# A linear attention and two MLPs on one core: one list scheduler for every queue, eight slices ahead of block 1, attention chunks 4 to 23 in one chain

## The chip, the core and the metric

The kernel runs on one core of a Trainium2 chip. The metric is the device time of one execution in microseconds (us). The core has TensorE (PE, its weight loads shown apart as PEld), VectorE (DVE), ScalarE (ACT), GpSimd (POOL), SyncE (SP, which here only issues transfers) and 16 DMA engines. Every engine runs its own list of instructions in the order in which they were put there; an instruction at the head of a list that waits for another engine holds everything behind it.

## What is computed

The reference, cut to what matters (B = 4, H = 8, S = 768, D = 64; 3072 tokens, d_model 512, d_ff 2048, all float32 in the reference):

```python
for t in range(S):                                   # attention with a decayed state per head
    state = gamma * state + outer(k[:, :, t], v[:, :, t])
    y[:, :, t] = scale * (q[:, :, t] @ state)
x = y as 3072 tokens x 512
h = x @ w_in;  g = h * sigmoid(1.702 * h);                       x = g @ w_out     # first MLP
h = x @ w_in2; g = max(h, 0) + alpha * min(h, 0);              out = g @ w_out2    # second MLP
```

The weights arrive as 64-bit floats. Each product is made of three fp32r products (high by high, low by high, high by low), so each weight is turned into a high and a low part first.

## The kernel before

**Work.** The 3072 tokens are 24 attention chunks of 128 and six blocks of 512. Each MLP's weights are 16 slices of 128 features, each with an `in` and an `out` half. Converting one half takes two ACT passes and four DVE passes over the raw words (`conv_words`, `conv_f32`), then an ACT cast and a DVE subtraction for each of its two pieces `wb` (`conv_hi`, `conv_lo`).

**First part.** `plain()` runs 32 steps; a step is 12 matmuls of 512 columns into `ph` (`mlp_h`), the gate and a high/low split of `g`, and 12 matmuls into four banks `py` (`mlp_y`, one step later). The order is: block 0 on the first LEAD slices, block 1 on all 16, block 0 on the rest. Block 0's partial sums are stored (`part`) and loaded again. Beside that run the conversion of the first MLP's weights, the storing of the pieces for the later part, the sums of pieces that the later part needs (`conv_sums`, `slice_sums`, `conv_split`) and attention chunks 0 to 15.

**Second part.** Blocks 2 to 5 of the first MLP and all of the second MLP are five pairs of blocks (`PAIRS`), computed with seven products in place of eight: 280 units of 6 matmuls (`h_unit`, banks `pa` and `pd`) and 280 chunks of 6 matmuls (`y_chunk`, banks `py`), the chunks 36 units behind. Weight pieces are loaded again from HBM, HRING = 6 units and YRING = 6 chunks ahead. The second MLP's weights are converted here, and attention chunks 16 to 23 are done.

**Attention turns.** From chunk 4 on, `half_step(o, new)` does the output of chunk `o` (32 matmuls of 64x64 into `px`) alternating with the scores and the state update of chunk `new` (32 matmuls into `sc` and `pu`). The table TURN says where; `None` stands for a side that is left out. A turn needs `v_scale(new)`, eight ACT multiplications of 128x64, and that needs the chunk's loads.

**Loads.** Everything but chunks 8 to 15 of attention, and the weights, goes to one of 82 slots of SBUF (`load_early`, four transfers of 256 KB a chunk, tile `early`). Raw weights and chunks 8 to 15 (RINGED) share a ring `ld` of five buffers of 512 KB: a load into it is issued when the load five places earlier has been used up.

**Order.** In the first part a list scheduler (`play`) sets the order of PE, DVE, ACT and SP together: each piece of work is a generator that yields an engine, a time, what it reads and what it writes; the scheduler keeps a clock for each engine, each slot and the DMA, and takes the piece that can start first, or one of a lower rank number that can start within 200 ns of it. In the second part only PE's order is written by hand; the other engines' order is left to the framework's own scheduler, with `tc.high_priority` for some pieces.

Of the kernel before, what the change touches and what calls it, by code (L numbers as in the profile page):

```python
# [35 lines left out]
LEAD = 5  # L36
LAG = 1
WARM = 30
# [4 lines left out]
HP = 300  # L43
HG = 100
# [21 lines left out]
YRING = 6  # L66
# [8 lines left out]
STORE_W = (24, 0.9)  # L75
# [11 lines left out]
def tile_linear_attention_two_mlps(ctx: ExitStack, tc, qk, kv, w1, w2, consts, alpha, out):  # L87
# [59 lines left out]
    chains, number, planning = [], counter(), [True]  # L147
# [54 lines left out]
    def start(gen, rank=0.0):  # L202
        if not planning[0]:
            with tc.high_priority(HG):
                for _ in gen:
                    pass
            return
        chain = [rank, next(number), gen, None]
        if go(chain):
            chains.append(chain)  # L210
# [125 lines left out]

    def conv_all(key):
        for part_ in (conv_words, conv_f32, conv_hi, conv_lo):
            yield from part_(key)

# [66 lines left out]
    def conv_sums(kind, layer, i):  # L407
        pair = (kind, layer, 2 * i), (kind, layer, 2 * i + 1)
        yield lambda: all(k in raw for k in pair)
# [33 lines left out]
    def conv_split(kind, layer, i):  # L443
        yield lambda: (kind, layer, i) in sums
        for name, s in zip(("s1", "s3"), sums.pop((kind, layer, i))):
            ws = []
            for part_ in halves(s):
                ws.append((yield from piece_hi(part_, s)))
# [30 lines left out]
    def v_scale(c):  # L479
        vt = loaded["kv", c][1]  # L480
# [132 lines left out]
    def half_psum(which, c):  # L613
        if c >= 4 * BT // C:
# [3 lines left out]
    def half_products(o, new):  # L618
# [51 lines left out]
        span = {32: 2100, 16: 1150}[len(turns)] / 2  # L670
# [18 lines left out]
    def half_step(o, new):  # L689
        if o is not None:  # L690
            yield lambda: ("a", o) in att and ("mid", o) in att
        if new is not None:
            yield lambda: ("v", new) in att
# [11 lines left out]
        start(half_rest(o, new), 0.1)  # L705
# [33 lines left out]
    def half_x(c):  # L739
        px, key = att.pop(("px", c))  # L740
        px = px.rearrange("p (n i) -> p n i", n=NP)
        t, i = divmod(c % (2 * BT // C), BT // C)
        if c < 2 * BT // C:
            x32 = att["x", c] = take("x32", (P, NP, C))
        for k in range(2):
            for d in range(2):
# [5 lines left out]
                if i == 0:  # L752
                    xl[k, d, t] = take("xl")
                yield V(240, [key], [xl[k, d, t]])
                x_out(xl[k, d, t][:, i * C:(i + 1) * C], px[:, n, :], c, n)
                if i == BT // C - 1:
                    ready.add(("xl", c // (2 * BT // C), k, d, t))
# [18 lines left out]
    def x_load(idx, t):  # L776
        assert ("x", idx) in stored
        for k in range(2):
            for d in range(2):
                xl[k, d, t] = take("xl")  # L780
                nc.sync.dma_start(out=xl[k, d, t], in_=xsd[idx][k, :, d, t])

    def x_prep(idx, n):
# [6 lines left out]
        if idx == 0:  # L790
            yield lambda: n == 0 or ("xp", n - 1) in ready
            yield lambda: all(("xl", 1, k, d, t) in ready for k in range(2) for d in range(2) for t in range(2 if n > 1 else 1))
        for k in range(2):
            if which == "t2":
                t1, t2 = xt[idx, "t1", k], xt[idx, "t2", k] = take("t1"), take("t2")
                yield from sub(t1, xl[k, 0, 1], xl[k, 0, 0])
                yield from sub(t2, xl[k, 1, 1], t1)
                give(xl.pop((k, 0, 0)))
            if which == "t3":
                xt[idx, "t3", k] = take("t3")  # L800
                yield from sub(xt[idx, "t3", k], xl[k, 1, 1], xl[k, 0, 1])
                give(xl.pop((k, 0, 1)))
            if which == "t4":
                xt[idx, "t4", k] = t = xt.pop((idx, "t2", k))
                yield from sub(t, xl[k, 1, 0], t)
                give(xl.pop((k, 1, 0)))
            if which[0] == "b":
                yield from x_split(idx, n, k, xl[k, int(which[1]) - 1, int(which[2]) - 1])
                if which == "b22":
                    give(xl.pop((k, 1, 1)))  # L810
# [4 lines left out]
        if idx == 0:  # L815
            ready.add(("xp", n))
# [7 lines left out]
    def gate(layer, ft, g, src):  # L824
        if layer == 1:
            nc.scalar.activation(out=g, in_=src, func=AF.Gelu_apprx_sigmoid)
            return
        t = take("t")
        nc.scalar.activation(out=t, in_=src, func=AF.Relu, scale=-1.0)  # L829
        nc.scalar.activation(out=g, in_=src, func=AF.Relu)  # L830
        nc.vector.scalar_tensor_tensor(  # L831
# [4 lines left out]
    def g_split(g, keep=False):  # L836
        gh, gl = take("gh", dtype=F32R), take("gl", dtype=F32R)
        nc.scalar.copy(out=gh, in_=g)  # L838
        nc.vector.tensor_tensor(out=gl, in0=g, in1=gh.bitcast(F32), op=ALU.subtract)  # L839
# [29 lines left out]
    def mlp_g(j, ft, ph, key):  # L869
        g = take("g")  # L870
        yield A(480, [key], [g])
        gate(1, ft, g, ph)
        gh, gl = take("gh", dtype=F32R), take("gl", dtype=F32R)
        yield A(505, [g], [gh])
        nc.scalar.copy(out=gh, in_=g)
        yield V(600, [g, gh], [gl])
        nc.vector.tensor_tensor(out=gl, in0=g, in1=gh.bitcast(F32), op=ALU.subtract)
        give(g)
        g_of[1, j, ft] = gh, gl
# [55 lines left out]
    def load_piece(ring, name, kind, layer, i, n):  # L935
# [7 lines left out]
        nc.sync.dma_start(out=dst, in_=src)  # L943
# [28 lines left out]
    def h_unit(u):  # L972
        quad, n = units[u]
        idx, q = divmod(quad, NQ)
        layer = PAIRS[idx][0]
        w = hw.popleft()
        if n == 0:
            chain[quad, "a"] = ps_h.tile([P, BT], F32, tag="h", name="pa")
            chain[quad, "d"] = ps_a.tile([P, BT], F32, tag="a", name="pd")
        ps = chain[quad, "d" if n % 2 else "a"]  # L980
        x = xo[idx, n][0]
        prods = [(part_, 0, k) for k in range(2) for part_ in range(2)] + [(0, 1, k) for k in range(2)]
        for m, (part_, low, k) in enumerate(prods):
# [8 lines left out]
        g = None  # L992
        with tc.high_priority(HP):
            if n in (0, 2, 3):
                chain[quad, n] = take("gw")
                nc.scalar.copy(out=chain[quad, n], in_=ps)  # L996
            elif n in (1, 4, 5):
                g = chain.pop((quad, {1: 0, 4: 3, 5: 2}[n]))
                nc.vector.tensor_tensor(out=g, in0=ps, in1=g, op=ALU.add)  # L999
        if g is not None:  # L1000
            t, odd = {1: (0, 0), 4: (1, 1), 5: (1, 0)}[n]
            with tc.high_priority(HG):
                gate(layer, 2 * q + odd, g, g)
            g_of[idx, t, 2 * q + odd] = g
        if n == 6:
            g = g_of[idx, 0, 2 * q + 1] = take("gw")
            with tc.high_priority(HP):
                gate(layer, 2 * q + 1, g, ps)
        if q == QORD[idx][-1] and idx + 1 < len(PAIRS):
            for _ in x_prep(idx + 1, n):  # L1010
                pass
# [3 lines left out]
    def y_split(c):  # L1015
        with tc.high_priority(HG):
            idx, grp, p, m = ychunks[c]
            f = 2 * QORD[idx][GQ * grp + m]
            b11, b12 = (idx, 0, f), (idx, 1, f)
            b21, b22 = (idx, 0, f + 1), (idx, 1, f + 1)  # L1020
            sub = lambda o, x, y: nc.vector.tensor_tensor(out=o, in0=x, in1=y, op=ALU.subtract)
            which = X_OF[p]
# [394 lines left out]
```

## Time and profile before

| | |
|---|---|
| three runs | 1039.66, 1042.46 (median), 1043.55 us |
| the profiled execution | 1041.78 us, of which the span from the first to the last instruction is 1040.0 us |
| TensorE | busy 1019.2 us (98%), mean granted clock 0.993 |
| VectorE, ScalarE | busy 862.7 us (83%), 677.4 us (65%) |
| DMA | 285.46 MB, 274 GB/s over the span |

The time outside the span is 1.8 us. A busy TensorE is not a TensorE at full rate: a matmul counts as busy from its start to its modelled end, also when the clock is halved. So the busy share alone does not say what is left; the rate at which matmuls follow each other, and the places where one waits, do.

### The profile page before, as it was taken

To read this page: it belongs to the slowest core of one execution; us is meant where nothing else is said; L and a number is where in the kernel's file an instruction comes from. 1 tells how busy PE (TensorE), PEld (TensorE's weight loads), DVE (VectorE), ACT (ScalarE), POOL (GpSimd) and SP (SyncE) were. 2 spreads that over 40 slices of the span, in tenths; PEclk is the share of its full clock that TensorE was granted. 3 is DMA by queue.
4 is the path that set the end of the run, shared out by engine and by line. 5 is a ranking of instruction groups with operands and counts; after the bars stand their busy time and mean duration, and the time that the engine had idled before them with its cause. 6 is when DMAs were issued, how large, how long until landed. Compare 5 with 4: busy or idle time off the path is not lost.

```text
span 1040.0 us, 19858 instructions
## 1 busy us (share of the span) xinstructions
PE 1019.2 (98%) x6910; PEld 842.8 (81%) x6910; DVE 862.7 (83%) x1711; ACT 677.4 (65%) x1407; POOL 2.8 (0%) x6
## 2 busy tenths in 40 slices
PE   8999989999999999999999999999999999999998
PEld 7788878787888888888788888788888888888886
DVE  5979979784559999999899999998677978677792
ACT  6958857556455886765776776775555855556740
POOL 1000000000000000000000000000000000000000
PEclk9999999999999999999999999999999999999999
DMA  9749999997846899999979898986686766775661
GB/s 350 238 146 378 382 350 328 373 312 265 275 135 204 283 314 374 352 391 375 358 246 341 311 318 323 323 290 207 219 283 211 217 215 191 227 250 172 193 202 61
DMA packets 144676, 285.46 MB, mean 274 GB/s; under 512 B 16192, under 2 KB 16576, under 8 KB 144576
## 3 DMA queue, kind: packets, MB, share of 16 engines
q1 hardware_dynamic: 144288, 283.84, 80.5%
q8 instruction: 55, 0.90, 0.4%
q10 hardware_dynamic: 288, 0.35, 0.1%
q14 instruction: 45, 0.37, 0.1%
HBM read 209.68 MB, written 74.45 MB: 273 GB/s over the span
## 4 chain that ended last, share of the span: by engine, by line
PE 84%; DMA 7%; DVE 4%; ACT 4%; issue 1%; SPq 0%; DVEq 0%; ACTq 0%
PE py L1058 34%; PE pa L984 20%; PE pd L984 15%; PE py L900 5%; PE ph L863 5%; DMA ld<-kv 2%; PE px L626 2%; ACT v L485 1%; DMA yw<-wcout 1%; ACT wb L356 1%; DMA wcin<-wb 1%; DMA xsd<-y 1%; DMA ld<-w 1%; DVE wb L361 1%; DVE gl L839 1%
## 5 line engine op out<-in xcount | busy, mean ns | idle before, releaser
L1058 PE MATMUL py<-gh,yw 128*128 128x512 f32 x1120 | 300.5, 390 | 0.0
L1058 PEld LDWEIGHTS py<-gh,yw 128*128 128x128 f32 x1120 | 210.6, 188 | 44.1 <-ACT gh L838 0.3
L984 PE MATMUL pa<-xo,hw 128*128 128x512 f32 x912 | 231.3, 390 | 0.0
L984 PEld LDWEIGHTS pa<-xo,hw 128*128 128x128 f32 x912 | 170.8, 188 | 35.7
L839 DVE TENSOR_TENSOR gl<-gw,gh 128x512 fp32r<-128x512 f32 x240 | 160.8, 687 | 37.2 <-ACT gh L838 33.1
L838 ACT CAST gh<-gw 128x512 fp32r<-128x512 f32 x240 | 145.5, 621 | 61.9 <-PE py L1058 29.9
L984 PE MATMUL pd<-xo,hw 128*128 128x512 f32 x684 | 173.8, 390 | 2.6 <-ACT gw L996 2.6
L1058 PE MATMUL py<-gl,yw 128*128 128x512 f32 x560 | 173.1, 390 | 1.3 <-DVE gl L839 1.3
L984 PEld LDWEIGHTS pd<-xo,hw 128*128 128x128 f32 x684 | 128.6, 188 | 29.9 <-ACT gw L996 3.0
L1058 PEld LDWEIGHTS py<-gl,yw 128*128 128x128 f32 x560 | 105.3, 188 | 23.5 <-DVE gl L839 1.7
L1072 DVE TENSOR_TENSOR yc<-py,yc 128x512 f32<-128x512 f32 x99 | 63.6, 683 | 25.3 <-PE py L1058 25.3
L831 DVE SCALAR_TENSOR_TENSOR gw<-t,nalpha,gw 128x512 f32<-128x512 f32 x96 | 71.2, 747 | 15.6 <-ACT gw L830 15.4
L829 ACT ACTIVATE t<-gw 128x512 f32<-128x512 f32 x72 | 45.5, 632 | 51.6 <-DVE gw L999 46.8
L863 PE MATMUL ph<-xhi,wb 128*128 128x512 f32 x256 | 65.8, 399 | 2.8 <-ACT wb L356 2.1
L900 PE MATMUL py<-gh,wb 128*128 128x512 f32 x256 | 66.0, 400 | 1.3 <-DVE wb L361 1.3
L999 DVE TENSOR_TENSOR gw<-pd,gw 128x512 f32<-128x512 f32 x80 | 54.8, 685 | 6.9 <-PE pd L984 6.8
L996 ACT COPY gw<-pa 128x512 f32<-128x512 f32 x80 | 46.6, 583 | 21.4 <-PE pa L984 20.8
L863 PEld LDWEIGHTS ph<-xhi,wb 128*128 128x128 f32 x256 | 48.4, 191 | 13.6 <-ACT wb L356 2.3
L900 PEld LDWEIGHTS py<-gh,wb 128*128 128x128 f32 x256 | 48.1, 192 | 12.4 <-DVE wb L361 1.8
L356 ACT CAST wb<-cvt 128x256 fp32r<-128x256 f32 x112 | 41.0, 403 | 25.1 <-DVE cvt L334 14.4
L361 DVE TENSOR_TENSOR wb<-s,wb 128x256 fp32r<-128x256 f32 x128 | 48.4, 420 | 10.5 <-ACT wb L356 10.5
L356 ACT CAST wb<-s 128x256 fp32r<-128x256 f32 x128 | 47.5, 403 | 13.0 <-DVE s L421 10.6
(107 smaller groups left out, 1368.0 us busy)
## 6 DMA issues: line engine op xcount, KB each, us to landing
hw<-wcin SPq DMA_DIRECT2D x266, 256.0 KB, 4.4
yw<-wcout SPq DMA_DIRECT2D x232, 256.0 KB, 3.7
ld<-w SPq DMA_DIRECT2D x64, 512.0 KB, 5.8
wcin<-wb SPq DMA_DIRECT2D x112, 256.0 KB, 5.6
wcout<-wb SPq DMA_DIRECT2D x88, 256.0 KB, 5.2
yw<-wo SPq DMA_DIRECT2D x48, 256.0 KB, 5.1
early<-kv SPq DMA_DIRECT2D x32, 256.0 KB, 5.4
early<-qk SPq DMA_DIRECT2D x32, 256.0 KB, 5.6
```

The costliest lines, as they stand in the source:

```text
L356: nc.scalar.copy(out=w[:, 0:256], in_=src)
L361: nc.vector.tensor_tensor(out=w[:, 256:], in0=src, in1=w[:, 0:256].bitcast(F32), op=ALU.subtract)
L831: nc.vector.scalar_tensor_tensor(out=g, in0=t, scalar=nalpha[:, ft:ft + 1], in1=g, op0=ALU.mult, op1=ALU.add)
L838: nc.scalar.copy(out=gh, in_=g)
L839: nc.vector.tensor_tensor(out=gl, in0=g, in1=gh.bitcast(F32), op=ALU.subtract)
L863: nc.tensor.matmul(out=ph, lhsT=cols(w, low, k), rhs=x[:, k, :], start=(n == 0), stop=(n == len(prods) - 1),)
L900: nc.tensor.matmul(out=py[e], lhsT=lhsT, rhs=g, start=(begin and seen[e] == 1), stop=(end and seen[e] == 3))
L984: nc.tensor.matmul(out=ps, lhsT=w[:, 256 * part_ + k * P:256 * part_ + (k + 1) * P], rhs=x[2 * k + low], start=(n in (0, 1, 3) and m == 0) ...
L996: nc.scalar.copy(out=chain[quad, n], in_=ps)
L999: nc.vector.tensor_tensor(out=g, in0=ps, in1=g, op=ALU.add)
L1058: nc.tensor.matmul(out=ps[e], lhsT=w[:, at:at + P], rhs=t, start=(fresh and seen[e] == 1), stop=(m == GQ - 1 and seen[e] == 3), skip_group ...
L1072: add_ = lambda o, x: nc.vector.tensor_tensor(out=o, in0=ps, in1=x, op=ALU.add)
```

## The change

- All queues of both parts are ordered by the one list scheduler: `h_out`, `gate`, `g_split`, `y_split`, `y_out` and the loads of the second part become generators with engines and times, or go through `dma()`, which keeps the scheduler's clock of the DMA; `plain` and `streamed` are one lead chain for PE. `high_priority` and the framework's order are gone.
- LEAD goes from 5 to 8.
- TURN has no `(x, None)`, `(None, y)` pair between chunk 4 and chunk 23 any more: 21 turns for 23.
- RINGED is empty: chunks 8 to 15 are loaded in slots too. From chunk 17 on a chunk's loads are issued 24 units ahead of its turn, not 14. YRING goes from 6 to 5.
- All eight `out` sums are made from the converted words (RAW_OUT), so `slice_sums` is not used. Sums and stores of the first MLP are due earlier. The second MLP's conversions begin before the second part, and wait for free slots (SPARE).
- At the start there are 10 small matmuls for 30, then 18 on a tile of zeros, and five of 512 columns ahead of the first step (FILL).

```diff
-LEAD = 5
+LEAD = 8
-WARM = 30
+WARM = 10
+FILL = 5
-YRING = 6
+YRING = 5
-SUMS_IN = (16, 24, 32, 38, 40, 43, 45, 46)
-SUMS_OUT = (12, 20, 28, 36, 41, 48, 50, 52)
-RAW_OUT = (0, 1, 2, 3, 4)
+SUMS_IN = (14, 17, 20, 23, 30, 34, 38, 41)
+SUMS_OUT = (15, 18, 21, 24, 32, 36, 40, 43)
+RAW_OUT = range(8)
-RINGED = range(8, 16)
+RINGED = ()
-W2_AT = [9 + 0.86 * m for m in range(18)] + [26 + 1.25 * m for m in range(14)]
-TURN = ((None, 4, 0), (4, 5, 2), (5, 6, 4), (6, 7, 5), (7, None, 7))
-TURN += ((None, 8, 35), (8, 9, 37), (9, 10, 38), (10, 11, 42), (11, 12, 44), (12, 13, 46), (13, 14, 48), (14, 15, 50))
-TURN += ((15, None, 52), (None, 16, 2), (16, 17, 6), (17, 18, 10), (18, 19, 14), (19, 20, 18), (20, 21, 27))
-TURN += ((21, 22, 30), (22, 23, 33), (23, None, 36))
-FETCH = 14
+W2_AT = [-2 + 1.4 * m for m in range(8)] + [10 + 1.3 * m for m in range(24)]
+TURN = ((None, 4, 0), (4, 5, 8), (5, 6, 10), (6, 7, 12), (7, 8, 14))
+TURN += ((8, 9, 34), (9, 10, 36), (10, 11, 39), (11, 12, 43), (12, 13, 45), (13, 14, 48), (14, 15, 50), (15, 16, 52))
+TURN += ((16, 17, 7), (17, 18, 10), (18, 19, 14), (19, 20, 18), (20, 21, 28), (21, 22, 31), (22, 23, 34), (23, None, 36))
+FETCH = 24
+SPARE = 13
...
     def conv_all(key):
+        if key[1] == 2:
+            yield lambda: len(free) >= SPARE and working[0] < 2
+            working[0] += 1
         for part_ in (conv_words, conv_f32, conv_hi, conv_lo):
             yield from part_(key)
...
-                nc.sync.dma_start(out=xl[k, d, t], in_=xsd[idx][k, :, d, t])
+                dma(xl[idx, k, d, t], xsd[idx][k, :, d, t], writes=[xl[idx, k, d, t]])
...
-        with tc.high_priority(HP):
-            if n in (0, 2, 3):
-                chain[quad, n] = take("gw")
-                nc.scalar.copy(out=chain[quad, n], in_=ps)
...
+        start(h_out(quad, n, ps, key), 0.0)
...
+    def h_out(quad, n, ps, key):
+        if n in (0, 2, 3):
+            g = take("gw")
+            yield A(480, [key], [g])
+            nc.scalar.copy(out=g, in_=ps)
+            chain[quad, n] = g
+            return
...
-            job(12 + m if ft < LEAD else STORE_W[0] + STORE_W[1] * (m - 10), store, (("in", "out")[n], 1, ft))
+            job(first + 1 if ft < LEAD else lead + 4 + 1.1 * (m - lead), store, (("in", "out")[n], 1, ft))
...
+        idle, key = bank("y3", "idle")
+        yield T(FILL * 220, [], [key])
+        for _ in range(FILL):
+            nc.tensor.matmul(out=idle, lhsT=warm[:, :P], rhs=warm, start=True, stop=True)
...
-    play(plain())
-    planning[0] = False
-    ordered.close()
-    ctx.enter_context(tc.manual_schedule(engines={mybir.EngineType.PE}))
...
+    def whole():
+        yield from plain()
+        yield from streamed()
+
+    play(whole())
```

How the order moves, at the places of which the next sections speak. TensorE where chunk 7 ends, before: the output of chunk 7 alone between two steps, and some 200 rows further on the same pattern with the scores and update of chunk 8 alone.

```order
L900 MATMUL py_734<-gl,wb 128x512
L626 MATMUL px<-early,hstate_82 64x64 x8
L626 MATMUL px<-a,v 64x64 x16
L626 MATMUL px<-early,mid 64x64 x8
L863 MATMUL ph<-xhi,wb 128x512 x8
L863 MATMUL ph<-xlo,wb 128x512 x4
L900 MATMUL py_731<-gh,wb 128x512
```

```order
L900 MATMUL py_1213<-gl,wb 128x512
L626 MATMUL sc<-ld 64x64 x16
L626 MATMUL pu<-v,ld 64x64 x16
L863 MATMUL ph<-xhi,wb 128x512 x8
L863 MATMUL ph<-xlo,wb 128x512 x4
L900 MATMUL py_1210<-gh,wb 128x512
```

TensorE where chunk 7 ends, in the changed kernel (the first rows of a turn of 64 matmuls, chunk 7's output alternating with chunk 8's scores, then its update; 12 matmuls of `py` and then the first `ph` of block 1 follow):

```order
L906 MATMUL py_647<-gl,wb 128x512
L876 MATMUL ph<-xhi,wb 128x512 x8
L876 MATMUL ph<-xlo,wb 128x512 x4
L629 MATMUL px<-early,hstate_82 64x64
L629 MATMUL sc<-early 64x64
L629 MATMUL px<-early,hstate_82 64x64
L629 MATMUL sc<-early 64x64
```

The two turns of 32 matmuls with steps between them have become one of 64, and it stands 12 `py` matmuls ahead of the step that reads chunk 7's result.

SP, the loads of chunks 10 to 12 before, among stores of weight pieces (`wcin`, `wo`, `wcout`):

```order
L196 DMA ld<-qk 128x1024
L196 DMA ld<-kv 128x1024
L196 DMA ld<-qk 128x1024
L196 DMA wo_133<-wb 128x512 x2
L196 DMA wcin_2_91<-wb 128x512 x4
L196 DMA ld<-kv 128x1024
L196 DMA ld<-qk 128x1024
L196 DMA wcin_6_95<-wb 128x512
L196 DMA wo_134<-wb 128x512 x2
L196 DMA ld<-kv 128x1024
```

The same queue in the changed kernel, the loads of chunks 11 and 12:

```order
L194 DMA early<-kv 128x512
L194 DMA early<-qk 128x512 x2
L194 DMA early<-kv 128x512
L194 DMA wo_133<-wb 128x512 x2
L194 DMA ld<-part 128x1024 x2
L194 DMA wcin_7_96<-wb 128x512 x2
L194 DMA wcout_4_109<-wb 128x512 x4
L194 DMA ld<-w 128x1024
L194 DMA early<-kv 128x512
L194 DMA early<-qk 128x512 x2
L194 DMA early<-kv 128x512
```

A chunk comes as four pieces of 256 KB in slots and not as two of 512 KB in the ring; the loads of the second MLP's weights (`ld<-w` here) already stand among them.

ACT in the second part, at the third pair of copies `yc<-py` of the second pair of blocks, before (`gw<-pd` empties the bank `pd`, into which TensorE's next products go; `wb` are weight pieces of the second MLP):

```order
L838 CAST gh<-gw 128x512
L996 COPY gw<-pd 128x512
L838 CAST gh<-gw 128x512
L772 CAST xo<-t_6918 128x512
L772 CAST xo<-t_6919 128x512
L1082 COPY yc<-py 128x512 x2
L826 ACTIVATE gw<-gw 128x512
L356 CAST wb<-cvt 128x256 x2
L996 COPY gw<-pd 128x512
L838 CAST gh<-gw 128x512
L772 CAST xo<-t_6928 128x512
L772 CAST xo<-t_6929 128x512
```

ACT at the same pair of copies in the changed kernel:

```order
L1009 COPY gw<-pd 128x512
L850 CAST gh<-gw 128x512
L1009 COPY gw<-pd 128x512
L776 CAST xo<-t_7023 128x512
L356 CAST wb<-s_6816 128x256 x2
L776 CAST xo<-t_6977 128x512
L850 CAST gh<-gw 128x512
L776 CAST xo<-t_7022 128x512
L834 ACTIVATE gw<-gw 128x512
L850 CAST gh<-gw 128x512
L834 ACTIVATE gw<-gw 128x512
L1106 COPY yc<-py 128x512 x2
```

The two emptyings `gw<-pd` stand ahead of the group of casts in the changed list; the weight pieces `wb` stand ahead of the copies, not between them and an emptying.

## Rows read from the trace of the kernel before

**Rows 1.** the page: busy time by engine, GB/s in 40 slices of 26 us

```profile
PE 1019.2 (98%) x6910; PEld 842.8 (81%) x6910; DVE 862.7 (83%) x1711; ACT 677.4 (65%) x1407; POOL 2.8 (0%) x6
...
GB/s 350 238 146 378 382 350 328 373 312 265 275 135 204 283 314 374 352 391 375 358 246 341 311 318 323 323 290 207 219 283 211 217 215 191 227 250 172 193 202 61
```

**Rows 2.** waits of TensorE: engine, line, releaser: us in total, times, longest

```profile
PE pu L626 <- ACT v L485: 4.1, 3, 1.7
...
PE pd L984 <- ACT gw L996: 2.6, 1, 2.6
...
PE py L900 <- DVE wb L361: 1.3, 1, 1.3
...
PE py L1058 <- DVE gl L839: 1.3, 1, 1.3
...
PE ph L863 <- DVE wb L361: 0.7, 1, 0.7
```

**Rows 3.** the chain that ended last, in order of time: start, us, what

```profile
70.79 2.72 PE ph L863 x12
...
985.72 50.33 PE py L1058 x222
```

**Rows 4.** attention turns (L626), each in its window: us, PE, PEld, PEclk, DMA, GB/s

```profile
135.70:138.60 2.90, 2.60 (x64) 2.40 (x64) 1.00 1.03 392
143.90:148.30 4.40, 3.04 (x128) 2.64 (x128) 1.00 1.06 403
150.90:157.30 6.40, 3.42 (x128) 3.16 (x128) 0.84 0.64 221
191.80:198.40 6.60, 3.64 (x128) 3.18 (x128) 0.83 1.03 376
211.90:214.30 2.40, 2.05 (x64) 1.95 (x64) 1.00 0.85 329
...
266.90:269.30 2.40, 2.02 (x128) 1.96 (x128) 1.00 0.74 249
```

**Rows 5.** busy time by stretch: us, PE, PEld, DVE, ACT, POOL, PEclk, DMA, GB/s

```profile
26.00:30.00 4.00, 4.00 (x21) 2.92 (x21) 3.51 (x9) 2.77 (x10) 0.00 (x0) 0.64 0.90 294
...
80.00:120.00 40.00, 40.00 (x178) 33.14 (x177) 39.75 (x103) 35.38 (x78) 0.00 (x0) 1.00 1.03 381
...
512.00:522.00 10.00, 7.45 (x26) 5.66 (x25) 8.24 (x14) 7.82 (x16) 0.00 (x0) 0.83 0.92 312
```

**Rows 6.** timeline of TensorE, first 30 us: start, us, what, idle before

```profile
1.05 4.54 PE L1253 MATMUL idle<-warm 128*128 128x192 bf16 x30 [1.05 <-DVE warm L1250]
6.36 1.16 PE L495 MATMUL sc<-early 64*128 64x128 f32 x16 [0.76 <-DMA early<-qk]
...
25.17 3.52 PE L863 MATMUL ph<-xhi,wb 128*128 128x512 f32 x8 [2.15 <-ACT wb L356]
```

**Rows 7.** waits of ScalarE

```profile
ACT v L485 <- DMA ld<-kv: 18.8, 6, 6.2
```

**Rows 8.** DMA issues: what, count, KB each, median us to landing

```profile
early<-qk SPq DMA_DIRECT2D x32, 256.0 KB, 5.6
...
ld<-qk SPq DMA_DIRECT2D x8, 512.0 KB, 6.6
```

**Rows 9.** timeline of ScalarE at 512 us

```profile
512.79 1.07 ACT L1082 COPY yc<-py 128x512 f32<-128x512 f32 x2 [0.83 <-PE py L1058]
...
514.28 0.71 ACT L356 CAST wb<-cvt 128x256 fp32r<-128x256 f32 x2
514.88 0.60 ACT L996 COPY gw<-pd 128x512 f32<-128x512 f32 x1
```

**Rows 10.** timeline of VectorE after chunk 5's output

```profile
45.77 0.69 DVE L712 TENSOR_TENSOR a<-sc,cst 128x512 f32<-128x512 f32 x1
...
46.84 1.12 DVE L576 SCALAR_TENSOR_TENSOR x<-px,cst 128x128 f32<-128x128 f32 x4
```

**Rows 11.** timeline of ScalarE there

```profile
47.99 0.62 ACT L600 CAST xhi<-x 128x512 fp32r<-128x512 f32 x1
```

More of the change, by code (lines that the diff above doesn't have):

```diff
@@ L408, in conv_sums @@
         pair = (kind, layer, 2 * i), (kind, layer, 2 * i + 1)
-        yield lambda: all(k in raw for k in pair)
+        yield lambda: all(k in raw for k in pair) and (layer == 1 or len(free) >= SPARE)
         a, b = (raw.pop(k) for k in pair)
@@ L870, in mlp_g @@
         g = take("g")
[L871 to L879, printed above, removed]
+        yield from gate(1, ft, g, ph, key)
+        g_of[1, j, ft] = yield from g_split(g)
     def mlp_y(layer, j, ft, begin, end, carry):
@@ L1005, in h_unit @@
[L1005 to L1011, printed above, removed]
+        start(h_out(quad, n, ps, key), 0.0)
+        if q == QORD[idx][-1] and idx + 1 < len(PAIRS):
+            start(x_prep(idx + 1, n), 0.3)
+    def h_out(quad, n, ps, key):
+        idx, q = divmod(quad, NQ)
+        layer = PAIRS[idx][0]
+        if n in (0, 2, 3):
[4 more added lines that the diff above has]
+            return
+        if n == 6:
+            g, t, odd = take("gw"), 0, 1
+            src = ps
+        else:
+            old = {1: 0, 4: 3, 5: 2}[n]
+            t, odd = {1: (0, 0), 4: (1, 1), 5: (1, 0)}[n]
+            yield lambda: (quad, old) in chain
+            g = src = chain.pop((quad, old))
+            yield V(600, [key, g], [g])
+            nc.vector.tensor_tensor(out=g, in0=ps, in1=g, op=ALU.add)
+            key = None
+        yield from gate(layer, 2 * q + odd, g, src, key)
+        g_of[idx, t, 2 * q + odd] = g
@@ new lines, in y_split, with sub @@
+        f = 2 * QORD[idx][GQ * grp + m]
+        b11, b12 = (idx, 0, f), (idx, 1, f)
+        b21, b22 = (idx, 0, f + 1), (idx, 1, f + 1)
+        yield lambda: p == 0 or ("ys", idx, f, p - 1) in ready
+        yield lambda: p > 2 or all(b in g_of for b in ((b11,), (b21,), (b11, b12, b21, b22))[p])
+        def sub(o, x, y):
+            yield V(600, [x, y], [o])
+            nc.vector.tensor_tensor(out=o, in0=x, in1=y, op=ALU.subtract)
+        which = X_OF[p]
+        if which == "t2":
+            t2 = take("t2")
+            yield from sub(g_of[b11], g_of[b12], g_of[b11])
+            yield from sub(t2, g_of[b22], g_of[b11])
+            yield from sub(g_of[b21], g_of[b21], t2)
+            ysplit[c] = yield from g_split(t2)
+        else:
@@ L1038, in tile_linear_attention_two_mlps @@
+        ready.add(("ys", idx, f, p))
     ych, acc = {}, {}
@@ L1155, in tile_linear_attention_two_mlps @@
         if new is not None:
-            if new >= 4 * per:
+            if new > 4 * per:
                 put_in = unit_job
@@ L1220, in run, with begin @@
             fn, args, _ = jobs[slot][i]
-            made = fn(*args)
-            if not inspect.isgenerator(made):
-                continue
-            if not planning[0]:
-                for _ in made:
-                    pass
-            elif fn in on_pe:
-                yield from made
-            else:
-                start(made, 0.24 if fn is conv_all and args[0] == ("in", 1, 0) else 10.0 + due(fn, args, slot))
+            yield from begin(fn, args, slot)
+    def begin(fn, args, slot):
+        made = fn(*args)
+        if not inspect.isgenerator(made):
+            return
+        if fn in on_pe:
+            yield from made
+        else:
+            start(made, 0.24 if fn is conv_all and args[0] == ("in", 1, 0) else 10.0 + due(fn, args, slot))
     o = NLEAD
```

250 lines of the change are left out of this document (126 added, 124 removed).

## The prediction

> **What bounds the kernel now.** I read the engine shares first: PE is busy 1019.2 of 1040.0 us, DVE 862.7, ACT 677.4 [rows 1]. So PE is the path, and the question is how much of its span is work at full rate. For that I read the chain of waits in order of time: a step's 12 matmuls of 512 columns take 2.72 us, 0.2267 each [rows 3]. The program has 32 steps of 24, 280 units of 6 and 280 chunks of 6, together 4128, so 935.7 us. Then the attention turns: one of 64 matmuls and one of 128 each occupy PE for 2.05 and 2.02 us [rows 4]. I take 2.1 with the switch; 23 turns are 48.3 us. The first step starts at 25.17 [rows 6]. 25.2 + 935.7 + 48.3 = 1009.2, but PE ends at 985.72 + 50.33 = 1036.05 [rows 3]: 26.8 us are waits and slow clock. Behind that the last additions and stores take 4.0 us, and 1.8 us lie outside the span. The profiled execution has 1041.8, the three runs a median of 1042.5; I reckon against the former and change nothing for the 0.7 between them.
>
> Where the 26.8 lie:
> - At the first step 8 matmuls take 3.52 us instead of 1.8 plus 0.2 of modelled end, with the granted clock at 0.64 in 26 to 30 us; PE had been idle for 2.15 us just before [rows 5, 6]. Loss 1.5.
> - In the first steps PE waits 0.7 and 1.3 for DVE's weight pieces [rows 2]. Loss 2.0.
> - Four turns with chunks from the ring are wide: against a window of 2.40 they take 0.5, 2.0, 4.0 and 4.2 more [rows 4]; two of them show 0.84 and 0.83 of the clock and the clock is halved past their ends, which I estimate at 0.7 each. Loss 12.1. The direct waits are 4.1 us for `v` [rows 2], and ACT, which makes `v`, waits 18.8 us in 6 times for the loads [rows 7].
> - In the second part PE waits 2.6 us for an emptying of `pd` by ACT and then has 0.83 of the clock over 10 us, 1.7 us lost; later 1.3 us for a split [rows 2, 5]. Loss 5.6.
> - The rest, 5.6, is spread in small pieces: refills of PE's pipeline after turns and waits, the handover between the parts.
>
> **Part by part.**
>
> *The chain without breaks.* The matmuls are the same in number. But a turn of 64 costs PE what a turn of 128 costs, 2.05 against 2.02 [rows 4]; only when output and scores alternate do they share the array. Two turns go: chunk 7 and 8 meet in one, 15 and 16 in one. That is 2 x 2.1 = 4.2 us on the path, with nothing that could hide it, since PE has no slack. This is the firmest term; its ends are 4.0 and 4.6.
>
> *The start.* The 30 small matmuls took 4.54 us, and the first scores waited for their load until 6.36 [rows 6]. Of the new ones ten cost 10 x 0.15 = 1.5; the 18 on zeros end before about 6.5 if the two row halves run side by side, as halves do in the turns, and near 9 if not. So 0 to 2.6, taken 0.2 (inside the spread rest below). The five matmuls of FILL, 1.1 us at 0.22 each, lie in the 2.15 us in which PE was idle and cost nothing while that gap lasts; without it, 1.1. They cut the idle stretch to some 1.1 us. The slow stretches followed idle stretches of 2.15 and 2.6 us; the waits of 1.3 us had none behind them [rows 2, 5]. So I count the 1.5 as gained; the ends are 0 and 1.5. The weight conversion ahead of the first step stands in the same order, so 25.17 stays.
>
> *LEAD = 8.* No matmul more or less. In 80 to 120 us, where a slice is converted per step beside stores and sums, DVE was busy 39.75 of 40 us and PE lost nothing [rows 5]; so the lead runs on the edge, now for eight steps with four full turns in it rather than five steps. New is that the turn of chunk 7 stands 12 `py` matmuls (2.72 us) ahead of block 1's first step, which reads its result; before, 24 stood there. After a turn the mask, the state and the scaling on DVE and the cast on ACT took from 45.77 to 48.61, 2.8 us [rows 10, 11], and the mask can't begin before the turn ends. 2.8 - 2.7 = 0.1 is the least wait, and a DVE at its limit adds a pass or two. Before, 2.0 was lost here; I take 3.0, with 0.1 and 7 as ends (the upper one: the idle stretch grows past 2 us and the slow clock follows).
>
> *Loads in slots, stores earlier.* What made the ring late is the DMA: 146 GB/s in the slice from 52 to 78 us, then 378, 382, 350 [rows 1], 381 over 80 to 120 us at a share of 1.03 [rows 5], which is all it gives. The ring holds loads back while the DMA is idle and adds them when it is full. In the changed order sums and stores fill the lull, and by the queue's own order 44.8 MB stand up to the last piece of chunk 9, 64.2 up to chunk 14, 69.2 up to chunk 16 (before: 62.1 up to chunk 15). At 370 GB/s without a pause that is 121, 174 and 187 us. By the sum the turns of these chunks start at 128, 177 and 192, plus the 3 lost in the lead. So the loads are in time by 6 to 10 us if DMA never idles, and late by a few if it idles for 10 us, as it did before for longer. A piece takes 5.6 us from issue to landing and a ring load 6.6 [rows 8]. I take 2.5 us lost in place of 12.1; the ends are 0 and 12. The Trainium skill (DMA: Bandwidth & Descriptors, section Where 436 GB/s comes from) gives about 358 GB/s as the limit of one core's share of HBM; by it chunk 14 would come at 179 and the sum would be some 2 us longer. The row of 381 GB/s over 40 us does not agree with that limit.
>
> *The second part by the list.* At 513 us ACT's list had two copies, a gate and two weight casts ahead of the emptying for which PE stood [rows 9]; that order was made without the times of the other engines. In the changed list the emptyings stand ahead of the casts there. DVE's share in the second part does not change but for 12 small sums (5 us in all) that go; they cost nothing on the path. I take 1.5 us lost in place of 5.6, ends 0 and 10: the list was computed from fixed times, and where a load is late the whole list behind it stands.
>
> *Sum.* 25.2 + 935.7 + 21 x 2.1 (44.1) + spread rest 4.5 + 0 + 3.0 + 2.5 + 1.5 = 1016.5 for PE's end; + 4.0 + 1.8 = 1022.3. As differences: -4.2 turns, -1.5 first step, +1.0 lead, -9.6 loads, -4.1 second part, -1.1 rest: -19.5. **1022 us.**
>
> **Rivals.**
> - *The loads are late all the same* (DMA full from the start, lull or not): the stage keeps the 12 us. For it speaks that 69.2 MB must now pass in the time of the 62.1 before; against it, the lull of 52 to 78 us. 1022 + 9.6 = 1032.
> - *Only the turns go.* The waits move and do not shrink: the lead waits more, the loads as before, the second part as before. 1041.8 - 4.2 = 1037.6. For it: DVE at 39.75 of 40; against it: each wait has a cause that the order touches.
> - *Slower: ACT's list stands for `v`.* `v_scale` of a chunk is put into ACT's list at a fixed place. When its load is late, ACT stands, and with it every gate and every emptying behind; before, that took 12.1 us for four turns, 3 each [rows 4, 7]. Sixteen chunks, 8 to 23, now come this way. If each were late like those: 16 x 3 = 48, less the 2.5 in the sum: 1022 + 46 = 1068. It decides from about 28 us in all, 1.7 per chunk, where the result passes 1047. Against it: chunks 16 to 23 came that way before, and the windows of their turns are plain (266.9 [rows 4]), and now they are fetched earlier.
> - *Better than forecast:* all three new waits near 0: 1015.
>
> **How the numbers follow.** Forecast (1017 to 1028) 0.56; better 0.08; late loads (1028 to 1036) 0.17; only the turns (1036 to 1042) 0.11; slower 0.08, of which 0.02 only a little. About 0.5%, 5.2 us, is what a measurement of this kernel can tell from no change; faster means under 1037.2. Faster: 0.56 + 0.08 + 0.17 + a quarter of 0.11 = 0.84; same: the rest of 0.11 and 0.02 = 0.10; slower 0.06. The range leaves out the slower case, most of the turns-only case and the edge of the better one: 1014 to 1036.
>
> **What would show it.** Turns of 128 with 2.4 us windows at all of chunks 8 to 16, and 21 of them: the chain and the loads right. A granted clock of 1.00 in 24 to 30 us: the filling right. A wait of `ph` for the cast of `x` near 77 us: the lead as reckoned. ACT waiting for `early<-kv` by more than a few us: late loads. No wait of `pd` for ACT in the second part: the list right. I would be wrong if PE waits in the second part, where it had almost none, add up to over 10 us, or if the first step starts later than 26 us.

## The result: 1028 us for 1022 forecast, and the profile after

The changed kernel takes 1028.16 us (median of four runs, 1026.24 to 1032.37) against 1041.26 for the kernel before; the ratio of the means is 0.9878, 95% interval 0.984 to 0.9916. So it is faster by 1.2%, inside the range of 1014 to 1036, and 6 us above the point. The profiled execution took 1027.75 us, where the sum of the forecast gave 1022.3; the span is 1025.7. Here is the sum again, with what each term became in that execution. It is taken from the starts of TensorE's matmuls: every distance over 0.2267 us between two matmuls of 512 columns, and for a turn the time from the last matmul ahead of it to the first one behind it. The waits of the lead are those up to 82 us, the second part is all behind 350 us, and the rest is what lies between and the small pieces.

| term | forecast us | measured us |
|---|---|---|
| first step starts | 25.2 | 25.4 |
| 4128 matmuls of 512 columns | 935.7 | 935.7 |
| 21 turns of 2.1 | 44.1 | 44.1 |
| turns wider than 2.1 (loads) | 2.5 | 6.8 |
| waits of the lead | 3.0 | 3.4 |
| second part | 1.5 | 0.3 |
| rest | 4.5 | 6.0 |
| last additions and stores | 4.0 | 3.9 |
| outside the span | 1.8 | 2.1 |

From the page of the changed kernel, TensorE's busy time and the transfer rate in 40 slices of 26 us, to lay beside [rows 1]:

```profile
PE 1010.3 (98%) x6913; PEld 834.5 (81%) x6913; DVE 867.2 (85%) x1700; ACT 675.3 (66%) x1407; POOL 2.8 (0%) x6
...
GB/s 345 293 402 308 356 360 344 364 190 209 383 343 256 220 290 389 331 351 386 258 299 322 294 268 384 276 262 155 215 223 321 194 226 160 190 242 259 148 124 192
```

The lull of the third slice is filled (402 in place of 146), and the ninth falls to 190 from 312. TensorE's waits in the changed kernel (engine, line, releaser: total, times, longest), beside [rows 2]:

```profile
PE sc L629 <- DMA early<-qk: 3.9, 3, 1.8
...
PE py L906 <- ACT wb L356: 1.1, 1, 1.1
PE ph L876 <- ACT wb L356: 1.0, 1, 1.0
...
PE ph L876 <- ACT xhi L603: 0.9, 1, 0.9
```

The waits for `v`, for an emptying of `pd` and for a split have gone. What leads now is a wait that was small in the kernel before, the scores of a turn (`sc`) for the q and k of their chunk. There it was:

```profile
PE sc L626 <- DMA ld<-qk: 1.2, 1, 1.2
```

The turns, each in its window (us, PE, PEld, PEclk, DMA share, GB/s), beside [rows 4]:

```profile
132.90:135.60 2.70, 2.23 (x128) 2.09 (x128) 1.00 1.03 385
...
152.30:156.10 3.80, 2.33 (x112) 2.17 (x112) 1.00 0.89 308
166.80:170.60 3.80, 2.37 (x128) 2.17 (x128) 1.00 1.02 377
175.80:179.10 3.30, 2.45 (x112) 2.24 (x112) 1.00 1.06 400
187.10:191.70 4.60, 2.40 (x128) 2.17 (x128) 1.00 0.97 346
196.90:199.40 2.50, 2.08 (x128) 1.96 (x128) 1.00 1.04 372
```

PE is busy for 2.1 to 2.5 us in windows of up to 4.6; the clock stays at 1.00. Four turns are still wide by 0.8 to 2.2 us each, those that bring the scores of chunks 11 to 14 and the output of the chunk before. With three that are wide by less (chunk 9 and 10 by 0.15 and 0.2, chunk 22 at 302 us by 0.6, where the profile shows no load waited for) the wide turns cost 6.8 us against 11.1 in the kernel before.

### The profile page after: what moved, and what is told of

Same layout as the page of the kernel before. It is cut to its first block, busy times and chain, and to the rows that moved or that the text cites. A ratio compares the mean times of both kernels' runs of the same rounds, so it can differ in the third digit from the quotient of the medians.

```text
span 1025.7 us, 19939 instructions
## 1 busy us (share of the span) xinstructions
PE 1010.3 (98%) x6913; PEld 834.5 (81%) x6913; DVE 867.2 (85%) x1700; ACT 675.3 (66%) x1407; POOL 2.8 (0%) x6
## 4 chain that ended last, share of the span: by engine, by line
PE 83%; DVE 6%; DMA 5%; ACT 4%; issue 1%; SPq 0%; DVEq 0%; ACTq 0%
PE py L1080 37%; PE pa L991 21%; PE pd L991 16%; DMA ld<-w 3%; PE py L906 2%; PE ph L876 2%; PE px L629 2%; DVE wb L361 2%; DMA early<-kv 1%; DMA early<-qk 1%; ACT v L488 1%; ACT cvr L306 1%; ACT wb L356 1%; ACT cvt L303 1%; DVE s L421 1%
## 5 line engine op out<-in xcount | busy, mean ns | idle before, releaser
L850 ACT CAST gh<-gw 128x512 fp32r<-128x512 f32 x240 | 145.1, 616 | 17.3 <-DVE gw L1038 11.9
L906 PE MATMUL py<-gh,wb 128*128 128x512 f32 x256 | 64.9, 395 | 2.1 <-ACT wb L356 1.1
L488 ACT ACTIVATE v<-early,cst 128x64 f32<-128x64 f32 x192 | 49.9, 336 | 14.2 <-DMA early<-kv 11.9
L834 ACT ACTIVATE gw<-gw 128x512 f32<-128x512 f32 x48 | 30.3, 630 | 36.9 <-DVE gw L1021 36.4
```

Of the source, the lines that this page charges most:

```text
L906: nc.tensor.matmul(out=py[e], lhsT=lhsT, rhs=g, start=(begin and seen[e] == 1), stop=(end and seen[e] == 3))
```

## Where the loads are late: e1 and e5

The forecast took the rate of the DMA engines as what paces the loads. SyncE's queue in the changed kernel shows another pace. Its order ahead of the widest turn (start, us, count; the pieces named `early` are the loads of chunk 14, whose turn begins at 187.1):

```profile
180.85 0.80 SPq L194 DMA_DIRECT2D wo<-wb  x2
182.19 0.84 SPq L194 DMA_DIRECT2D wcin<-wb  x2
183.09 0.45 SPq L194 DMA_DIRECT2D early<-kv  x1
183.59 0.99 SPq L194 DMA_DIRECT2D early<-qk  x2
```

q and k are issued 3.5 us before TensorE wants them, and the page gives 5.7 us from issue to landing. The same reckoning for the other turns: for chunk 10 the issue is 7.3 us ahead and the turn is 0.2 wide, for 11 it is 5.2 and 1.4, for 12 4.6 and 1.35, for 14 3.6 and 2.2, for 15 8.8 and nothing. (Chunk 13's q and k, 6.8 ahead, took 6.5 to land; its turn is 0.8 wide, with a wait of 0.2 for VectorE's `xl` in it.) The loads stand three half-steps ahead of their turn in SyncE's list (a half-step is 12 matmuls of 512 columns, 2.72 us), behind stores, and SyncE itself waits before it issues a store. The largest group of its waits between 120 and 200 us (total, times, longest):

```profile
SPq L194 <- DVE wb L361: 17.0, 17, 3.0
```

So two theories stand against each other: the place in the list, or a DMA that has no more to give in this stretch.

**e1** moves the loads of chunks 10 to 14.

```
- job(at - (4 if new < 2 * per else 3), load_early, new)
+ ahead = {10: 6, 11: 6, 12: 6, 13: 5, 14: 5}
+ job(at - (4 if new < 2 * per else ahead.get(new, 3)), load_early, new)
```

> The changed kernel with the loads of chunks 10 to 12 put six half-steps ahead of their turn and those of 13 and 14 five, in place of three; nothing else is edited (the list follows). In the changed kernel seven turns are wider than 2.1 us, by 6.8 us together, and TensorE waits in three of them for early<-qk. Theory 'place': a load is put too late in SyncE's list, behind stores for which SyncE itself waits for VectorE; then the turns of chunks 10 to 14 fall to about 2.1 to 2.3 us, the excess falls from 6.8 to 1 to 2.5, and the span from 1025.7 to 1020 to 1022. Rival 'full': the DMA gives all that it has from 120 to 200 us, so an earlier load only makes something else later: excess plus new waits for weight pieces stay at 6 to 8 us together, and the span at 1024 to 1028.

Measured: ratio 0.9866 (0.9847 to 0.9886), no difference from 0.9878 that can be measured; the span of the profiled execution 1024.3. The turns of chunks 10 to 16 all take 2.1 us. But chunk 9's turn takes 7.4. SyncE's order around it in e1 (start, us, count):

```profile
123.02 0.38 SPq L194 DMA_DIRECT2D early<-kv  x1
...
130.52 0.33 SPq L194 DMA_DIRECT2D early<-kv  x1
...
132.46 0.33 SPq L194 DMA_DIRECT2D early<-kv  x1
```

ScalarE's scaling for it in e1:

```profile
136.27 2.02 ACT L488 ACTIVATE v<-early,cst 128x64 f32<-128x64 f32 x8
```

TensorE's longest wait in e1:

```profile
PE sc L629 <- ACT v L488: 3.6, 1, 3.6
```

And the turn in its window:

```profile
133.40:141.00 7.60, 3.63 (x128) 3.48 (x128) 0.80 1.01 374
```

Six half-steps ahead, chunk 10's load (123.02) has passed chunk 9's (130.52, in the changed kernel 126.41). Chunk 9's last piece is issued at 132.5 and `v` is begun at 136.3, nearly three microseconds after the turn should start, and behind the wait the window shows 0.80 of the clock. The excess went from 6.8 to 5.5, all of it at one place. By its numbers the run lies nearer to 'full', whose span of 1024 to 1028 it meets and whose 6 to 8 us it nearly does; by its turns, of which 10 to 14 are all plain as 'place' said, it speaks for the place. e1 leaves that open, and the next run decides it.

**e5** takes chunk 9 along.

```
- ahead = {10: 6, 11: 6, 12: 6, 13: 5, 14: 5}
+ ahead = {9: 6, 10: 6, 11: 6, 12: 6, 13: 5, 14: 5}
```

> The changed kernel with the loads of chunks 9 to 12 six half-steps ahead of their turn and of 13 and 14 five (three before). In the run that did so for 10 to 14 alone, chunk 10's load passed chunk 9's in SyncE's list: the turns of chunks 10 to 14 became plain (2.1 us), but chunk 9's load was issued at 130.5 in place of 126.4 us and its turn took 7.4 us. Theory 'place': with 9 moved too all turns up to chunk 16 are between 2.1 and 2.4 us, the excess of all turns is under 1 us (6.8 in the changed kernel), and the span is 1018.5 to 1020.5. Rival 'full': the DMA is at its limit in 120 to 200 us, so the 4 to 6 us come back at another load (chunk 8's neighbour, or pieces of weights for which TensorE waits), and the span stays at 1023 to 1026.

Measured: 1023.39 us median, ratio 0.9828 (0.9809 to 0.9847), span 1019.9. The excess of all turns is 1.05 us, as 'place' said but for a hair; one turn, chunk 11's, is wide by 0.56, more than it allowed. Two of the turns in e5, those of chunks 9 and 14, each in its window:

```profile
133.10:135.60 2.50, 2.10 (x128) 1.96 (x128) 1.00 1.05 415
...
183.00:185.50 2.50, 2.10 (x128) 1.96 (x128) 1.00 1.04 366
```

The stretch of 120 to 200 us (us, PE, PEld, DVE, ACT, POOL, PEclk, DMA share, GB/s) in e5:

```profile
120.00:200.00 80.00, 79.52 (x1206) 65.78 (x1208) 72.49 (x195) 58.31 (x163) 0.00 (x0) 1.00 1.03 380
```

The same stretch in the changed kernel:

```profile
120.00:200.00 80.00, 75.09 (x1119) 61.70 (x1118) 70.39 (x189) 55.68 (x153) 0.00 (x0) 1.00 0.99 353
```

With the loads earlier the same engines move 380 GB/s where they moved 353, and TensorE is busy for 4.4 us more of the stretch. (The share adds up the times of packets over 16 engines and can pass 1.) The DMA was busy in the changed kernel, but not at its end. SyncE now waits less for VectorE (same view, e5, 120 to 200 us):

```profile
SPq L194 <- DVE wb L361: 6.0, 14, 0.9
```

Chunk 14's q and k are issued at 172.5 us for a turn at 183.1. So it was the place in the list: a fixed distance of three half-steps, about 8 us by TensorE, less what SyncE stands for stores, against 5.7 us of load. (Both sides of that moved in e5, the distance and SyncE's waits; how much each gave is not shown.) The Trainium skill (DMA: Bandwidth & Descriptors, section Anatomy of one DMA — SWDGE (gpsimd) path) says, where it treats transfers issued by GpSimd, that a wait for a semaphore is done by the issuing engine's sequencer before the transfer is sent, not by the DMA engines. The rows of SyncE, which issues the transfers here, agree: 17.0 us of such waits on stores, with the loads behind them in the same queue. The Trainium skill's limit of about 358 GB/s that the prediction weighed (DMA: Bandwidth & Descriptors, section Where 436 GB/s comes from) is passed here by 380 over 80 us.

**e8** goes at the planner instead. Its list reckons a load at 2.05 us fixed and 0.67 for the bytes; the trace has 5.6 to 5.7. On top of e5:

```
- fixed = (3900 if t < 1000 else 2800) if t < 6000 else 2050 if writes else 1500
+ fixed = (3900 if t < 1000 else 2800) if t < 6000 else 4900 if writes else 1500
```

> As the run with chunks 9 to 14 loaded ahead, and the list told a load time nearer to the one in the trace: 4.9 us fixed in place of 2.05 (with 0.67 for the transfer 5.6, the median from issue to landing). Theory 'fixed times': ScalarE's waits for ld<-w and early<-kv (14.0 and 11.9 us in the changed kernel) fall by half, since the list now puts other work ahead of them; TensorE's own waits fall by 0 to 1 us. Rival 'list follows TensorE': the places of the loads in SyncE's list hang on TensorE's steps and not on that figure, so ScalarE's waits fall by less than 3 us and the span is the same within 0.5.

Measured: ratio 0.9823 (0.9804 to 0.9843), beside 0.9828 no difference; span of the profiled execution 1022.3. ScalarE's waits for loads in e8:

```profile
ACT v L488 <- DMA early<-kv: 15.0, 4, 5.2
ACT cvt L303 <- DMA ld<-w: 4.8, 7, 1.2
```

And in e5:

```profile
ACT cvt L303 <- DMA ld<-w: 11.6, 7, 4.6
ACT v L488 <- DMA early<-kv: 6.7, 4, 3.5
```

The waits have changed places, 18.3 us in e5 and 19.8 in e8: the list puts other work ahead of a weight that it knows to be late, and stands for `v` instead. TensorE loses 2 us less at the start (its wait at 47 us for a weight cast goes) and 4.6 us more at the turns of chunks 7 (65 us), 15 and 16. Neither theory is quite right; that the time doesn't move is the rival's, the fall in the waits for weights is the first one's.

## What the merged turns are worth: e3

```
- (7, 8, 14)   ... (15, 16, 52)
+ (7, None, 14), (None, 8, 14)   ... (15, None, 52), (None, 16, 52)
```

> The changed kernel with its two merged turns cut apart again at the same places: output of chunk 7 and scores of chunk 8, output of 15 and scores of 16, each as a turn of its own. Theory 'turns': 23 turns, two more windows of 2.1 us with TensorE at full length, so plus 4.0 to 4.4 us. Rival 'slack': the cut turns give DMA, VectorE and ScalarE 4 us more ahead of the later turns and steps, so part of the waits there (6.8 us of wide turns, 3 us of waits in the lead) goes and the sum is plus 1 to 3.

Measured: ratio 0.9972 (0.9956 to 0.9988) against 0.9878, span 1033.7: 8.0 us more, and neither theory said so much. The two pairs of cut turns and the widest turn:

```profile
75.50:79.70 4.20, 3.74 (x128) 3.65 (x128) 1.00 0.90 312
...
191.40:197.80 6.40, 3.26 (x128) 2.99 (x128) 0.84 0.93 296
211.40:215.60 4.20, 3.78 (x128) 3.65 (x128) 1.00 0.39 115
```

A pair takes 3.80 us where the merged turn takes 2.12, so the cut costs 2 x 1.68 = 3.4 us directly, a fifth less than the 4.2 reckoned for turns that stand apart as they did before. The other turns are wider by 3.9 us together: chunk 14's q and k are issued at 189.0 for a turn at 191.5, only 2.5 us ahead, and SyncE waits 22.6 us for the same weight pieces where it waited 17.0. The slack that the rival hoped for was not used: a list made anew put the loads closer to their turns. Why it did so is not settled; the issue time shows the mechanism of e1 and e5 at work at the widest turn, not that it makes up the whole of the 3.9 us.

## What the five matmuls ahead of the first step are worth: e2

```
- FILL = 5
+ FILL = 0
```

> The changed kernel without the five matmuls ahead of the first step (FILL = 0). The forecast counted 1.5 us for them: theory 'fill' expects the idle stretch ahead of the first step back at about 2.1 us, the granted clock of 26 to 30 us back at 0.6 to 0.7, the first step's first eight matmuls at about 3.5 us in place of 2.1, and the span longer by 1.4 to 1.7. Rival 'warm': it is the other new matmuls on zeros at the start, or the closer order, that keep the clock: 1.00 in 26 to 30 us also without the five, and a span within 0.4 us of the changed kernel's.

Measured: ratio 0.992 (0.9895 to 0.9944), span 1027.3. The later turns moved as well with the list made anew (chunk 12's takes 6.2 us in e2), and the interval overlaps the change's, so the price is read at the first step and not from the times. The first step in e2 (start, us, count, idle before):

```profile
25.13 2.77 PE L876 MATMUL ph<-xhi,wb 128*128 128x512 f32 x8 [2.15 <-ACT wb L356]
27.70 1.91 PE L876 MATMUL ph<-xlo,wb 128*128 128x512 f32 x4
```

And the stretch of 26 to 30 us in e2 (the clock is the third number from the end):

```profile
26.00:30.00 4.00, 4.00 (x22) 2.77 (x22) 3.47 (x9) 2.90 (x10) 0.00 (x0) 0.57 0.72 222
```

The first step in the changed kernel:

```profile
25.37 2.11 PE L876 MATMUL ph<-xhi,wb 128*128 128x512 f32 x8 [0.96 <-ACT wb L356]
27.32 1.07 PE L876 MATMUL ph<-xlo,wb 128*128 128x512 f32 x4
```

And its stretch of 26 to 30 us:

```profile
26.00:30.00 4.00, 4.00 (x68) 3.31 (x67) 3.81 (x11) 3.97 (x13) 0.00 (x0) 1.00 0.68 219
```

Idle for 2.15 us as before [rows 6], the first step runs at half clock again; after the five matmuls and 0.96 us of idling it does not. From the first matmul to the turn behind the step it is 4.4 us in e2 (25.13 to 29.54) and 2.95 in the changed kernel (25.37 to 28.32): 1.46 us, as forecast. Net it is 1.2, as the first step comes 0.24 us earlier without the five. By the turn at 75 us 0.8 is left, since part is taken up by shorter waits in the lead.

## What the list does in the second part: e4, e7, e9

Here the forecast put 4.1 us, of 5.6 lost before. In the changed kernel TensorE loses 0.3 us behind 350 us, and the stretch at 510 us, which held the wait and the slow clock [rows 5], is full:

```profile
510.00:520.00 10.00, 10.00 (x46) 8.29 (x45) 9.59 (x19) 9.91 (x20) 0.00 (x0) 1.00 0.77 260
```

To learn whether that is the list's, the second part was handed back to the framework's order by priorities, cut to its core:

```
- play(whole())
+ play(first_part())
+ planning[0] = False
+ ordered.close()
+ ctx.enter_context(tc.manual_schedule(engines={mybir.EngineType.PE}))
+ for _ in streamed():
+     pass
...
  def start(gen, rank=0.0):
+     if not planning[0]:
+         with tc.high_priority(HP if rank == 0.0 else HG):
+             for step_ in gen:
...
```

e4 gave the priority 300 to all that follows a unit or a chunk, its gates and stores too, and 100 to splits and the making of `x`. e7 is e4 with `YRING = 6` in place of 5, the loads of second-layer pieces in flight. e9 gives each operation the priority that it had in the kernel before, with six in flight and chunks fetched 14 units ahead.

> The changed kernel with the second part (from the 280 units on) handed back to the framework's order by priorities on ScalarE, VectorE and SyncE, and the conversion of the second weights at the slots of the kernel before; the first part stays by the list. Theory 'list': the waits of TensorE in the second part come back, 4 to 7 us of them against 0.3, with at least one stretch of granted clock under 1. Rival 'chance': the two long waits of the kernel before (2.7 and 1.5 us) came from where its order happened to stand, and another order by the same rule has 0 to 2 us of them.

> As the run with the second part in the framework's order (where the second part lost 26.6 us), with six loads of second-layer weight pieces in flight in place of five, as the kernel before had. There 10.6 us of TensorE's waits were for these loads and 4.2 us for a gate of ScalarE. Theory 'ring': the waits for the loads go (under 2 us), those for ScalarE stay (3 to 6 us), and the span is 1030 to 1036, as far above the changed kernel as the kernel before stood in this part. Rival 'order': the loads are late because they stand behind others in SyncE's order, so a sixth in flight changes little and the span stays at 1046 to 1052.

> The changed kernel with its second part rebuilt closer to the kernel before: the framework's order on ScalarE, VectorE and SyncE with the priorities of the kernel before at each operation (emptyings 300, gates and splits 100, stores, loads and the making of the next x without one), six pieces of second-layer weights in flight, the second weights at the old slots, chunks 17 to 23 fetched 14 units ahead in place of 24. In the two runs before, gates, stores and the next x had the priority too, and the second part lost 27 and 30 us against 0.3 in the changed kernel and 6.3 in the kernel before. Theory 'list': it loses 4 to 8 us, so the span is 1029.5 to 1033.5, and the whole of the 6 us in this part is the list's. Rival 'both': the framework's order fits only together with the first part's old order, so 15 us or more are lost here too (span over 1040), and the old order's 6.3 us can't be put down to it alone.

Measured: ratios 1.014 (1.0123 to 1.0156), 1.0154 (1.0096 to 1.0212) and 0.9961 (0.9939 to 0.9984); spans 1052.0, 1052.3 and 1033.2. TensorE's waits from 240 us on, in e4:

```profile
PE py L1087 <- DMA yw<-wcout: 7.6, 3, 3.2
PE pa L998 <- ACT gw L847: 4.2, 1, 4.2
PE py L1087 <- DMA yw<-wo: 3.0, 2, 2.8
```

In e7:

```profile
PE pd L998 <- DMA hw<-wcin: 10.2, 3, 4.1
PE py L1087 <- ACT gh L857: 7.9, 2, 5.4
```

In e9:

```profile
PE pd L1000 <- ACT gw L1019: 2.5, 1, 2.5
```

Neither theory of e4 had so much: it loses 26.6 us behind 350 us. The sixth load in flight only moved the waits from the second layer's pieces (`yw`) to the first layer's (`hw`), so e7's "ring" falls. e4 and e7 say nothing on the change, since their priorities were not those of the kernel before. Between them and e9 lie 19 us of span, and e7 and e9 have the same six loads in flight; they differ in the priorities and in the fetching of chunks 17 to 23. The long waits of e7 lie between 452 and 683 us, behind the last of these chunks' turns at 309 us, so the priorities are the likelier cause; the fetching was not undone alone. e9 does speak. Its span lies at the upper end of theory 'list' (1029.5 to 1033.5), far from 'both', and it has the very wait of the kernel before: ScalarE's order at 507 us:

```profile
507.39 1.07 ACT L1120 COPY yc<-py 128x512 f32<-128x512 f32 x2 [0.83 <-PE py L1092]
508.35 0.64 ACT L843 ACTIVATE gw<-gw 128x512 f32<-128x512 f32 x1
508.88 0.71 ACT L365 CAST wb<-cvt 128x256 fp32r<-128x256 f32 x2
509.48 0.59 ACT L1019 COPY gw<-pd 128x512 f32<-128x512 f32 x1
```

And the stretch around it:

```profile
506.00:516.00 10.00, 7.45 (x26) 5.63 (x26) 8.08 (x13) 7.92 (x17) 0.00 (x0) 0.83 0.90 320
```

Two copies, a gate and two casts ahead of the emptying, as in [rows 9]; 7.45 us of PE in 10 and 0.83 of the clock, as in [rows 5]. From 250 us on it loses 7.5 us outside the turns, as the kernel before does, and the changed kernel 1.4: 6.1 us are the list's (with the weights' slots, the fetching and the sixth load, which were undone with it).

## The lead: e6

The forecast reckoned 0.1 us or more, about 1 with a pass of VectorE, for block 1's first step behind chunk 7's output. The changed kernel around 81 us (VectorE makes `x`, ScalarE casts it, TensorE waits):

```profile
79.56 1.12 DVE L579 SCALAR_TENSOR_TENSOR x<-px,cst 128x128 f32<-128x128 f32 x4
...
80.71 0.62 ACT L603 CAST xhi<-x 128x512 fp32r<-128x512 f32 x1 [2.61 <-DVE x L579]
...
81.38 1.89 PE L876 MATMUL ph<-xhi,wb 128*128 128x512 f32 x7 [0.88 <-ACT xhi L603]
```

e6 is e5 with the two turns ahead of it a half-step earlier:

```
- (6, 7, 12), (7, 8, 14)
+ (6, 7, 11), (7, 8, 13)
```

> As the run with chunks 9 to 14 loaded ahead, and the turns of chunks 6|7 and 7|8 one half-step earlier each (at 11 and 13 in place of 12 and 14), so that 24 matmuls of py stand between chunk 7's output and block 1's first step in place of 12. The forecast's term for the lead was 3.0 us, of which it put about 1 on this one wait (measured 1.04 at 80 us, ph waiting for the cast of x). Theory 'distance': that wait goes (under 0.2) and the span is 0.5 to 1.0 less than without the edit. Rival 'edge': VectorE is the limit there (39.4 of 40 us busy), so the wait shows up elsewhere between 40 and 120 us and the span is the same within 0.4.

Measured: ratio 0.9824 (0.9802 to 0.9847) beside e5's 0.9828, no difference that can be measured. The wait at 80 us is gone; in its place the turn of chunk 7, now at 64.9 us, is wider by 0.65, and the span of the profiled execution is 2.7 us longer, at turns that were plain in e5. The rival holds in this: the microsecond is not won by moving the turn.

## Why the prediction was right, and which term was mis-sized

Right in sign, in the range, and in most of the steps:

- **The turns.** 21 of them, 44.1 us; two fewer. As the kernel before had its turns apart, -4.2 is what the sum lost; e3 puts the direct price at 3.4 where cut turns follow each other.
- **The first step.** -1.5 forecast; e2 shows 1.46 gross and 1.2 net. With the five matmuls the clock stays up, without them it falls, as forecast. That the length of the idle stretch decides, as the prediction read it from stretches of 2.15 and 2.6 us, is not shown: the two other slow stretches of the kernel before, at 155 and 196 us, followed idle stretches of 1.7 and 1.4 (with others of 0.9 and 1.2 within 4 us before), and in e7 TensorE stood for 3.55 us ahead of 480.9 us and its clock stayed at 1.00.
- **The lead.** 3.0 forecast, 3.4 found, with the named wait of `ph` for the cast of `x` (at 80 us and not 77, 1.0 us).
- **The second part.** 1.5 forecast, 0.3 found, where the kernel before lost 6.3 by the same count; so the gain was 6 and not 4. e9 brings the loss back with the order.
- **ScalarE's list standing for `v`,** the rival on the slower side. ScalarE did stand, 11.9 us in 7 times for `early<-kv`, but TensorE waited for q and k and not for `v`. e1 shows the price where it does decide: 5.3 us at one turn.
- **The rest** was 1.5 us more: waits of 0.9 us at 146 us for a gate and of 1.1 at 234 us for the last step's cast were in no term. With the lead (0.4 more) and the second part (1.2 less) it cancels for the most part, which is luck.

No run undid LEAD = 8, the empty ring or the earlier sums and stores by itself. The fall of the wide turns from 11.1 to 6.8 us is what they gave together; how it divides among them stays open.

The mis-sized term is *the loads*: 2.5 forecast, 6.8 found (with the 0.6 at 302 us), 4.3 of the 5.4 us between sum and result. The step that failed is the one that divided the megabytes up to each chunk's load by 370 GB/s "without a pause" and got chunk 14 at 174 us. Its q and k were issued at 183.6. The 370 were not met: over the first 131 us the DMA moved 341 GB/s and over the first 187 us 344, so the 44.8 MB up to chunk 9 had passed 10 us, and the 64.2 MB up to chunk 14 nearly 13 us, after the times reckoned. That lag alone does not make the turns late: e5 has the same one at 131 us (340 GB/s), and its turns are plain. Nor was the rate a bound, as e5 shows with 380 GB/s from 120 to 200 us; that 381 is all the DMA gives, as the prediction has it, no run shows (403 in a window of [rows 4], 415 in one of e5). What decided was the load's place in SyncE's order, three half-steps ahead of the turn and behind stores that wait for VectorE. That order was at hand before the result was: it stood in the changed kernel, as a distance of three half-steps, to be laid beside the 5.6 us of a load and SyncE's own waits.

The rival "the loads are late all the same" came true in part, by another cause than its own (a full DMA). With that cause removed, in e5, the profiled execution took 1021.7 us with 1.05 us of wide turns. e5 beats both kernels: 0.9828 of the kernel before, where the change has 0.9878, and each of its four runs (1021.68 to 1023.98 us) is under each of the change's.

## What to carry to other kernels

A load that shares a queue with stores can be paced by the waits of what stands ahead of it and not by bandwidth: compare issue time and time of need with the time from issue to landing, and try the load's place in the order first. Moving one load past others moves them back, so the neighbours need the same shift (e1 against e5). A list made from fixed times was worth 6 us in the second part, where it put the emptying of a bank, for which TensorE stood, ahead of casts; an order by priorities can hang on how they are set (e7 against e9, 19 us, not taken apart from the fetching).

## What the runs showed of the hardware that was not expected

- Two turns of 64 matmuls of 64 x 64 right behind each other take 3.80 us in e3, 1.9 each, where the merged turn of 128, which alternates two chunks, takes 2.12. Apart, a turn of 64 took 2.1 too (57 us in the kernel before).
- An idle stretch of TensorE did not tell by its length whether a slow one followed: half clock came behind 1.7 and 1.4 us in the kernel before (155 and 196 us), and none behind 3.55 and 2.48 us in e7 (481 and 538 us).
- A transfer share of 0.99 at 353 GB/s did not mean a full DMA: the same stretch moved 380 GB/s at 1.03 in e5.
